# The head of a fused layer-norm, MLP and long-convolution kernel: activations rounded ahead of weights, three short matmuls, one filter block moved

## The chip, the cores and the metric

The kernel runs on one core of a Trainium2 chip. A core has a matrix engine (TensorE, PE in the profile, with its weight loads shown as PEld), a vector engine (DVE), a scalar engine (ACT), a general engine (POOL) and a sequencer for transfers (SP). Each works through its own instructions in order, and they wait for each other through semaphores. Data lie in the on-chip buffer, in the accumulators of TensorE (PSUM), or in DRAM; transfers are issued by SP, ACT or POOL. The metric is device time of one execution in microseconds, lower is better; before the change it is 369.86 us, the median of three runs (369.53 to 370.65).

## The reference

```python
x  = A_q                                            # 1 x 2048 x 448
xn = layernorm(x)
# A: short convolution over k (4 taps), times v, then a causal convolution of length 2048 by FFT
k_shift = sum(k_pad[:, t:t+S] * shift_k[:, 3 - t] for t in range(4))
kv = k_shift * v
y  = irfft(rfft(kv, 2S) * rfft(ssm_k, 2S))[:S] + kv * ssm_D
a  = xn * y
# B: dense, Mish, dense
h   = xn @ w1 + b1                                  # 448 -> 1792
act = h * tanh(softplus(h))
b   = act @ w2                                      # 1792 -> 448
out = x + a + b
```

All is in 32-bit floating point.

## The kernel before

**Matrix products in two parts.** TensorE takes operands rounded to a shorter format. Each operand is kept as a rounded part (names ending in h: XH, w1h, w2h, ach) and the remainder (XL, w1l, w2l, acl). ACT makes the rounded part by a cast, DVE makes the remainder by a subtraction. A product is the sum of three: rounded with rounded (hh), remainder of x with rounded w (hl), rounded x with remainder of w (lh). D = 448 is 3.5 blocks of 128, so for w1 the half block left over holds the remainder of w1 in the other 64 rows of `w1h[:, 3]` and adds two matmuls (th and tl). One half of a pair is thus 11 matmuls, and a pair 22.

**The MLP's loops.** The 2048 rows are cut in 8 chunks of 256, and the 1792 columns in 7 pairs of 128. The 56 pairs (chunk, column pair), numbered i, go through one pipeline of half steps s. An even half step, s = 2i, holds the first product of pair i (`g1_mm`, L486). An odd one holds its activation (`mish`, L494 and the splitting at L80 and L81) and the second product of the pair two before (`g2_mm`, twelve matmuls, L511 to L513). In the first chunk the weights are also loaded and split: column pair p of w1 in half step 2p - 2 (`w1_split`: L346 on ACT, L351 and L353 on DVE), that of w2 in half step 2p + 3 (`w2_split`).

**The convolution.** Its FFT is done by small matrix products. The filter is cut in 8 blocks h. A block is loaded (`h_load`, L117), goes through eight matmuls that take a stretch of the matrix engine (`f1_mm`, L131), is folded on ACT and DVE (`f1_fold`: L137, L138, L140) and is stored to DRAM (`f1_out`, L146). The table `H_AT` says in which half step the matmuls of each block but the head's stand. The head's block is block 1 (`H_HEAD`). The products of k and v follow in `KV_AT`, and second stages later.

**Order.** The program's order is written by hand (`manual_schedule`): `at(s, f)` puts work ahead of the matmuls of half step s, `after(s, f)` behind them; each engine takes its share in that order. Tiles come from pools with a fixed number of buffers: `kr` four, `x` seven, `pc` (PSUM) two, `st` two. A new tile waits until the buffer that it takes is free, and transfers share eight semaphores, so a transfer can wait for an older one that had the same semaphore.

**The head** (L635 to L680) comes before half step 0. TensorE does four matmuls of zeros (`WARM`, L643) while the first rows of q come in, these are normalized on DVE and POOL, transposed by TensorE (L446) into PSUM, and split: ACT casts XH (L458), DVE subtracts XL (L456). The first column pair of w1 comes in two halves of 128 columns (L652), one issued by ACT and one by SP, and is split in two halves. ACT first casts the first half of w1, then XH; DVE does the first half's remainder, then XL. Block 1 of the filter is loaded by ACT's queue at the start, block 2 by SP's; block 1's matmuls stand in half step 1, between the products of pair 0 and pair 1.

Of the kernel before, what the change touches and what calls it, by code (L numbers as in the profile page):

```python
# [14 lines left out]
S, D, F = 2048, 448, 1792  # L15
# [7 lines left out]

G2_LAG = 2
H_HEAD = 1
H_AT = {2: 5, 3: 9, 0: 12, 4: 16, 5: 20, 6: 26, 7: 32}
KV_AT = (24, 29, 34, 39, 44, 50, 55, 59)
POOL_H = {20: (0, 2)}
H0_AT = 63
# [4 lines left out]
NT_AT = {"q": -5, "x": -1, "stats": -2, "flush": 0, "row": (4, 8), "norm": (7, 10), "split": (8, 11)}  # L34
WARM = 4
WARM_N = 448


@with_exitstack
def tile_kernel(ctx: ExitStack, tc, q, qT, k, v, sk, hT, sD, w1, b1, w2, c_f1, c_id, c_g, c_gi, c_i2, out):  # L40
    nc = tc.nc
# [15 lines left out]
    Dh = dp.tile([NO * 16, 32, D], F32, name="Dh")  # L57
# [25 lines left out]
    def pc():  # L83
        return pcp.tile([128, 2, 512], F32, name="pc")
# [10 lines left out]
    plan, plan2 = {}, {}  # L95

    def at(slot, fn, *args):
        plan.setdefault(int(slot), []).append((fn, args))

    def after(slot, fn, *args):  # L100
        plan2.setdefault(int(slot), []).append((fn, args))
# [5 lines left out]
    HT, KR, VT, KV, PP, PS, ST, SD = {}, {}, {}, {}, {}, {}, {}, []  # L107

    def xt():
        return sp1.tile([128, 2, D], F32, name="x", bufs=7)  # L110

    def kr():
        return sp1.tile([128, 4, CH], F32, name="kr", bufs=4)

    def h_load(g, eng=None):
        HT[g] = xt()
        (eng or nc.sync).dma_start(HT[g], hT[:, 2 * g:2 * g + 2])  # L117
        if g == 0:
            dt = xt()[0:1, 0]
            nc.sync.dma_start(dt, sD)  # L120
            SD.append(dt)
# [217 lines left out]
    RW = {}  # L339
# [5 lines left out]
    def w1_hi(p, a=0, b=256):  # L345
        nc.scalar.copy(w1h[:, :, 256 * p + a:256 * p + b], RW["1", p][:, :, a:b])  # L346

    def w1_lo(p, a=0, b=256, engs=(V, V)):
        fs, rw = slice(256 * p + a, 256 * p + b), RW["1", p][:, :, a:b]
        if engs[0]:  # L350
            engs[0].tensor_sub(w1l[:, :, fs], rw[:, 0:3], w1h[:, 0:3, fs])  # L351
        if engs[1]:
            engs[1].tensor_sub(w1h[64:128, 3, fs], rw[64:128, 3], w1h[64:128, 3, fs])  # L353
# [3 lines left out]
        w1_lo(p)  # L357

    def w2_load(p):
        RW["2", p] = rw = kr().rearrange("p a b -> p (a b)")[:, :2 * D].rearrange("p (a b) -> p a b", a=2)  # L360
        nc.sync.dma_start(rw, w2[:, 2 * p:2 * p + 2])

    def w2_split(p):
# [16 lines left out]
    def ln_parts(c):  # L380
        st = mp.tile([128, 2, 6], F32, name="bst", bufs=2)
        ve = mp.tile([128, 2], F32, name="ve", bufs=2)
        if c < NT:
            XN[c] = xn = xn_tile().rearrange("p a b -> p (a b)").rearrange("p (j d) -> p j d", j=2)
        eng = nc.gpsimd if 0 < c < NCHUNK - 1 else V

        def stats(jj):
            V.bn_stats(st[:, jj], Q[c][:, jj])

        def aggr(jj):  # L390
            V.bn_aggr(mv[:, 2 * c + jj], st[:, jj])

        def eps(a, b):
            V.tensor_scalar(ve[:, a:b], mv[:, 2 * c + a:2 * c + b, 1], EPS, None, op0=ALU.add)  # L394

        def power(a, b):
            nc.gpsimd.tensor_tensor(rs(c)[:, a:b], ve[:, a:b], mhalf[:, a:b], op=ALU.pow)  # L397

        def norm(jj):
            j = 2 * c + jj  # L400
            eng.tensor_scalar(xn[:, jj, :D], Q[c][:, jj], mv[:, j, 0:1], rs(c)[:, jj:jj + 1],  # L401
                              op0=ALU.subtract, op1=ALU.mult)

        def tail(a, b):
            eng.tensor_copy(xn[:, a:b, D:], xn[:, a:b, D - 64:D])

        return stats, aggr, eps, power, norm, tail
# [36 lines left out]
    def transposes(c, jj, p):  # L444
        for kt in range(4):
            nc.tensor.transpose(p[:, 128 * kt:128 * kt + 128], XN[c][:, jj, 128 * kt:128 * kt + 128], ident)  # L446
# [5 lines left out]
    def x_split(c, jj, p, lo):  # L452
        x = p.rearrange("p (a b) -> p a b", a=4)
        h, l = (t[:, :, 128 * jj:128 * jj + 128] for t in XS[c])
        if lo:
            V.tensor_sub(l, x, h)  # L456
        else:
            nc.scalar.copy(h, x)  # L458
# [14 lines left out]
    def g1_mm(i):  # L473
        c, p = pairs[i]
        XH, XL = XS[c]
        ps = g1p.tile([128, 2, CH], F32, name="pg1")
        for n in range(2):
            f = 2 * p + n
            fs = slice(128 * f, 128 * f + 128)
            mm = []  # L480
            hh, hl, lh = ([(w[:, kt, fs], x[:, kt]) for kt in range(3)] for w, x in ((w1h, XH), (w1h, XL), (w1l, XH)))
            th, tl = ((w1h[:, 3, fs], x[:, 3]) for x in (XH, XL))

            mm = hh + hl + lh + [th, tl] if i == 0 and n else hh + lh + [th] + hl + [tl]
            for n_, (l, r) in enumerate(mm):
                nc.tensor.matmul(ps[:, n], l, r, start=n_ == 0, stop=n_ == len(mm) - 1)  # L486
        P1[i] = ps
# [38 lines left out]
    def mlp_slot(s):  # L526
        i, half = divmod(s, 2)
        n = len(pairs)
        j = i - G2_LAG
        if half == 0:  # L530
            if i < n:
                c, p = pairs[i]
                if c + 1 < NT:
                    if p == 0:
                        ln_load(c + 1)
                    if p == (3 if c in (0, 2) else 2):
                        ln_stats(c + 1)
                    if c == 0:
                        dv(len(drip))
                    if p == NP - 1:  # L540
                        ln_T(c + 1, 1)
                g1_mm(i)
        else:
            if i < n:
                c, p = pairs[i]
                if p == NP - 2 and c + 1 < NT:
                    ln_T(c + 1, 0)
                mish(i)
            if 0 <= j < n - 1:
                g2_mm(j)  # L550
            elif j == n - 1:
                for jj in range(2):
                    g2_mm(j, (jj,))
                    g2_evac(pairs[j][0], (jj,))
# [3 lines left out]
    nslots = 2 * (len(pairs) + G2_LAG)  # L558

    for g, t in H_AT.items():  # L560
        if g != 2:
            at(t - 5 if t > 7 else t - 3, h_load, g)
        if g == 0:
            after(t - 2, lambda: V.tensor_add(HT[0][0:1, 0], HT[0][0:1, 0], SD.pop()))
        at(t, f1_mm, HT, g, "h")
        if t in POOL_H:
            after(t, taps_pool, *POOL_H[t])
        after(t, f1_fold, g, "h")
        at(t + 3, f1_out, Dh, g, "h", nc.gpsimd if t < 12 else nc.scalar)

    at(12, lambda: nc.sync.dma_start(skb, sk.partition_broadcast(128)))
    for g in range(-2, 0):
# [13 lines left out]
    for p in range(NP):  # L586
        if p >= 2:
            at(max(2 * p - 5, 0), w1_load, p)
        if p >= 1:
            at(2 * p - 2, w1_split, p)  # L590
        p and at(2 * p + (1 if p < 5 else 0), w2_load, p)
        after(2 * (p + G2_LAG) - 1, w2_split, p)

    for o in range(NO):
        s, d = OCT_AT[0] + OCT_AT[1] * o, OCT_AT[1]
        h = s - 1 if o else H0_AT
# [23 lines left out]
    for c in range(NT, NCHUNK):  # L620
        b = 2 * NP * (c - 1) + (1 if c == NT else 0)
# [16 lines left out]
    wz = cp.tile([128, 8], F32, name="wz")  # L638
# [3 lines left out]
    for _ in range(WARM):  # L642
        nc.tensor.matmul(warm[0:8, 0:WARM_N], wz, wz[:, 0:1].to_broadcast([128, WARM_N]), start=True, stop=True)  # L643

# [5 lines left out]
    nc.scalar.dma_start(ident, c_id)  # L650
    for n, eng in enumerate((nc.scalar, nc.sync)):
        eng.dma_start(RW["1", 0][:, :, 128 * n:128 * n + 128], w1[0, :, :, 128 * n:128 * n + 128])  # L652
    h_load(H_HEAD, nc.scalar)
    nc.scalar.dma_start(f1, c_f1)
    w1_load(1)
    nc.sync.dma_start(b1t, b1)
    w2_load(0)
    h_load(2)
    stats, aggr, eps, power, norm, tail = ln_parts(0)
    for jj in range(2):  # L660
        stats(jj)
        aggr(jj)
        eps(jj, jj + 1)
        power(jj, jj + 1)
    w1_hi(0, 0, 128)
    ps = [g2p.tile([128, 512], F32, name="pg2") for _ in range(2)]
    x_tiles(0)
    for jj in range(2):
        norm(jj)
        tail(jj, jj + 1)  # L670
        transposes(0, jj, ps[jj])
        x_split(0, jj, ps[jj], 0)
    w1_lo(0, 0, 128)
    w1_hi(0, 128, 256)
    x_split(0, 0, ps[0], 1)
    x_split(0, 1, ps[1], 1)
    w1_lo(0, 128, 256)
    plan.setdefault(1, []).insert(0, (f1_mm, (HT, H_HEAD, "h")))
    plan2.setdefault(1, []).append((f1_fold, (H_HEAD, "h")))
    plan.setdefault(4, []).insert(0, (f1_out, (Dh, H_HEAD, "h", nc.gpsimd)))  # L680
    for s in range(nslots):
        j = s // 2 - G2_LAG - 1
        if s % 2 == 0 and j >= 0 and pairs[j][1] == NP - 1:
# [76 lines left out]
```

## Time and profile before

| | |
|---|---|
| median of three runs | 369.86 us |
| profiled execution | 370.36 us |
| its span, first to last instruction | 368.5 us |
| TensorE busy | 358.9 us, 97% |
| DVE busy | 268.1 us, 73% |
| ACT busy | 166.6 us, 45% |
| first product (L486) starts | 9.32 us |
| last 3.5 us of the span | no matmul |

In the profile a row of the timeline gives start, duration, engine, line, operation, written tile and read tiles, their shapes, the number of merged instructions, and in brackets the idle time before and what ended it. Matmuls overlap: one of 256 columns lasts 0.28 us in the records while the next starts 0.118 us after it. Rows of waits give the waiting engine, tile and line, who released it, total us, count, and the longest. The granted clock is a share of TensorE's full clock.

### The profile page before, as it was taken

How to read it: one execution, taken by the hardware profiler on the slowest of the kernel's cores; microseconds unless marked ns; L12 is line 12 of the kernel's file. 1: busy time of each engine (PE TensorE's matmuls, PEld its weight loads, DVE VectorE, ACT ScalarE, POOL GpSimd, SP SyncE). 2: the span in 40 equal slices, each digit the busy share in tenths (PEclk: the TensorE clock that was granted, in tenths of full speed). 3: DMA queues.
4: the chain of work that ended last, by engine and by line, in shares of the span. 5: the costliest groups of instructions: out<-in, count | busy, mean ns of one | idle time of the engine just before them, and what ended most of it. 6: DMA issues, size and time to landing. Idle time of an engine off the chain costs nothing.

```text
span 368.5 us, 7457 instructions
## 1 busy us (share of the span) xinstructions
PE 358.9 (97%) x3104; PEld 291.7 (79%) x3104; DVE 268.1 (73%) x368; ACT 166.6 (45%) x277; POOL 71.0 (19%) x65
## 2 busy tenths in 40 slices
PE   6989999999999999999999999999999999999996
PEld 1878879888789889889886666666666889889885
DVE  4698767899999898699525773777666644997752
ACT  3668454243342532433436663655656444135450
POOL 2015300750226420904000020000010005103020
PEclk9899999999999999999999999999999999999999
DMA  6888998848589157552888888998898387959656
GB/s 218 317 233 308 362 348 230 246 148 276 150 224 302 51 151 206 164 137 46 225 241 276 265 210 213 307 245 221 290 259 220 59 251 242 408 212 287 116 63 136
DMA packets 33508, 81.69 MB, mean 222 GB/s; under 512 B 3266, under 2 KB 20291, under 8 KB 33475
## 3 DMA queue, kind: packets, MB, share of 16 engines
q1 hardware_dynamic: 21506, 46.45, 37.9%
q10 hardware_dynamic: 9056, 20.09, 22.4%
q0 software_dynamic: 2912, 14.69, 13.8%
q8 instruction: 24, 0.39, 0.4%
q14 instruction: 10, 0.07, 0.1%
HBM read 52.77 MB, written 28.45 MB: 220 GB/s over the span
## 4 chain that ended last, share of the span: by engine, by line
PE 53%; DVE 2%; ACT 1%; ACTq 1%; issue 0%
PE pg L486 20%; PE pg L511 7%; PE pc L214 7%; PE pg L513 7%; PE pg L512 7%; PE pc L257 4%; PE pc L314 2%; ACTq L268 1%; DVE x L178 1%; PE pc L131 1%; DVE x L181 0%; ACT qe L265 0%; ACT a L494 0%; ACT hs L225 0%; DVE qt L518 0%
## 5 line engine op out<-in xcount | busy, mean ns | idle before, releaser
L494 ACT ACTIVATE a<-pg,b1t 128x256 f32<-128x256 f32 x112 | 47.1, 472 | 109.8 <-PE pg L486 96.3
L486 PE MATMUL pg<-XH,w1h 128*128 128x256 f32 x448 | 91.6, 286 | 1.7 <-ACT XH L458 1.5
L486 PEld LDWEIGHTS pg<-XH,w1h 128*128 128x128 f32 x448 | 70.3, 189 | 19.5 <-issue 16.5
L511 PE MATMUL pg<-w2h,ach 128*128 128x448 f32 x224 | 83.3, 372 | 0.0
L81 DVE TENSOR_TENSOR acl<-a,ach 128x512 fp32r<-128x512 f32 x56 | 39.1, 698 | 59.0 <-ACT ach L80 59.0
L512 PE MATMUL pg<-w2l,ach 128*128 128x448 f32 x224 | 81.3, 363 | 0.5 <-DVE w2l L81 0.5
L513 PE MATMUL pg<-w2h,acl 128*128 128x448 f32 x224 | 81.4, 363 | 0.0
L486 PE MATMUL pg<-XL,w1h 128*128 128x256 f32 x448 | 70.5, 280 | 0.2 <-DVE XL L456 0.2
L486 PEld LDWEIGHTS pg<-XL,w1h 128*128 128x128 f32 x448 | 60.3, 190 | 0.4 <-DVE XL L456 0.4
L486 PE MATMUL pg<-XH,w1l 128*128 128x256 f32 x336 | 57.3, 279 | 1.4 <-DVE w1l L351 1.4
L511 PEld LDWEIGHTS pg<-w2h,ach 128*128 128x128 f32 x224 | 42.0, 187 | 15.1 <-issue 12.2
L486 PEld LDWEIGHTS pg<-XH,w1l 128*128 128x128 f32 x336 | 47.2, 189 | 1.6 <-DVE w1l L351 1.6
L512 PEld LDWEIGHTS pg<-w2l,ach 128*128 128x128 f32 x224 | 42.1, 188 | 3.2 <-DVE w2l L81 0.8
L513 PEld LDWEIGHTS pg<-w2h,acl 128*128 128x128 f32 x224 | 42.1, 188 | 2.7
L80 ACT CAST ach<-a 128x512 fp32r<-128x512 f32 x56 | 34.7, 620 | 1.8
L161 POOL TENSOR_TENSOR x<-kr,skb 128x896 f32<-128x896 f32 x8 | 17.0, 2130 | 78.0 <-DVE x L160 53.8
L178 DVE TENSOR_TENSOR x<-x 128x896 f32<-128x896 f32 x24 | 26.3, 1096 | 2.7 <-POOL x L161 2.2
L397 POOL TENSOR_TENSOR mv<-ve,mhalf 128x2 f32<-128x2 f32 x3 | 3.7, 1249 | 97.9 <-DVE ve L394 97.9
L138 DVE TENSOR_TENSOR st<-pc,st 128x896 f32<-128x896 f32 x16 | 17.4, 1089 | 6.0 <-ACT st L137 5.3
L137 ACT COPY st<-pc 128x896 f32<-128x896 f32 x16 | 14.5, 906 | 15.7 <-PE pc L131 13.0
L401 POOL TENSOR_SCALAR xn<-qt,mv,rstd 128x448 f32<-128x448 f32 x8 | 20.7, 2591 | 0.4
L265 ACT COPY qe<-pc 128x896 f32<-128x896 f32 x16 | 13.8, 912 | 12.0 <-PE pc L257 11.8
(76 smaller groups left out, 399.6 us busy)
## 6 DMA issues: line engine op xcount, KB each, us to landing
Dkv<-st ACTq DMA_DIRECT2D x16, 448.0 KB, 6.2
ah<-Dh SPq DMA_DIRECT2D x8, 896.0 KB, 7.6
av<-Dkv SPq DMA_DIRECT2D x8, 896.0 KB, 6.7
E<-qe ACTq DMA_DIRECT2D x16, 448.0 KB, 5.6
e<-E POOLq DMA_DIRECT2D x8, 896.0 KB, 8.1
kr<-in_k_dram SPq DMA_DIRECT2D x10, 448.0 KB, 6.5
Dh<-st ACTq DMA_DIRECT2D x10, 448.0 KB, 5.3
x<-in_v_dram SPq DMA_DIRECT2D x8, 448.0 KB, 4.0
```

The lines of the kernel that those rows point to most:

```text
L80: nc.scalar.copy(h, raw)
L81: V.tensor_sub(l, raw, h)
L138: V.tensor_add(st[:, 0], e, st[:, 1])
L161: nc.gpsimd.tensor_mul(o, KR[g - u // 2], skb[:, u:u + 1].to_broadcast([128, 2, D]))
L178: V.tensor_add(KV[g], KV[g], o)
L214: nc.tensor.matmul(p[32 * t:32 * t + 32, r, :D], g[rs, t, c], a[rs, t], start=True, stop=True, tile_position=(64 * r, 32 * t))
L401: eng.tensor_scalar(xn[:, jj, :D], Q[c][:, jj], mv[:, j, 0:1], rs(c)[:, jj:jj + 1], op0=ALU.subtract, op1=ALU.mult)
L486: nc.tensor.matmul(ps[:, n], l, r, start=n_ == 0, stop=n_ == len(mm) - 1)
L494: nc.scalar.activation(a[:, n], ps[:, n], AF.Mish, bias=b1t[:, 2 * p + n:2 * p + n + 1])
L511: nc.tensor.matmul(ps, ah[:, n, cs], w2h[:, f], start=f == 0, stop=False)
L512: nc.tensor.matmul(ps, ah[:, n, cs], w2l[:, f], start=False, stop=False)
L513: nc.tensor.matmul(ps, al[:, n, cs], w2h[:, f], start=False, stop=f == NF - 1)
```

## The change

Four things move, and one is added.

- In the head XH is cast ahead of w1's first half on ACT, and XL comes ahead of w1's remainders on DVE. The first half of pair 0 takes the order hh, hl, lh that only the second half had.
- Three matmuls of zeros, of 224 columns, are put between the transposes and the first product (`FILL`, `FILL_N`). They write a `pc` tile that nothing reads.
- Block 1 is loaded by SP, where block 2 was; its matmuls stand in half step 3 instead of 1, its fold at the end of half step 3, its store in half step 5 instead of 4.
- Block 2 goes from half step 5 to 6, and is loaded in half step 3 instead of in the head; the stores of blocks 2 and 3 are issued two half steps behind their matmuls and not three.
- The loads of the last two pieces of w2 (p of 5 and 6) take buffers of the `x` pool, the others those of `kr`.

```diff
-H_AT = {2: 5, 3: 9, 0: 12, 4: 16, 5: 20, 6: 26, 7: 32}
+H_AT = {2: 6, 3: 9, 0: 12, 4: 16, 5: 20, 6: 26, 7: 32}
...
+FILL = 3
+FILL_N = 224
...
     def w2_load(p):
-        RW["2", p] = rw = kr().rearrange("p a b -> p (a b)")[:, :2 * D].rearrange("p (a b) -> p a b", a=2)
+        RW["2", p] = rw = xt() if p > 4 else kr().rearrange("p a b -> p (a b)")[:, :2 * D].rearrange("p (a b) -> p a b", a=2)
         nc.sync.dma_start(rw, w2[:, 2 * p:2 * p + 2])
...
-            mm = hh + hl + lh + [th, tl] if i == 0 and n else hh + lh + [th] + hl + [tl]
+            mm = hh + hl + lh + [th, tl] if i == 0 else hh + lh + [th] + hl + [tl]
...
-        if g != 2:
+        if g != H_HEAD:
             at(t - 5 if t > 7 else t - 3, h_load, g)
...
-        at(t + 3, f1_out, Dh, g, "h", nc.gpsimd if t < 12 else nc.scalar)
+        at(t + (2 if t < 12 else 3), f1_out, Dh, g, "h", nc.gpsimd if t < 12 else nc.scalar)
...
-    h_load(H_HEAD, nc.scalar)
     nc.scalar.dma_start(f1, c_f1)
     w1_load(1)
     nc.sync.dma_start(b1t, b1)
     w2_load(0)
-    h_load(2)
+    h_load(H_HEAD)
...
-    w1_hi(0, 0, 128)
     ps = [g2p.tile([128, 512], F32, name="pg2") for _ in range(2)]
     x_tiles(0)
...
         transposes(0, jj, ps[jj])
         x_split(0, jj, ps[jj], 0)
+    fill = pc()[:, 0]
+    for _ in range(FILL):
+        nc.tensor.matmul(fill[0:8, 0:FILL_N], wz, wz[:, 0:1].to_broadcast([128, FILL_N]), start=True, stop=True)
+    w1_hi(0, 0, 128)
+    x_split(0, 0, ps[0], 1)
+    x_split(0, 1, ps[1], 1)
     w1_lo(0, 0, 128)
     w1_hi(0, 128, 256)
-    x_split(0, 0, ps[0], 1)
-    x_split(0, 1, ps[1], 1)
     w1_lo(0, 128, 256)
-    plan.setdefault(1, []).insert(0, (f1_mm, (HT, H_HEAD, "h")))
-    plan2.setdefault(1, []).append((f1_fold, (H_HEAD, "h")))
-    plan.setdefault(4, []).insert(0, (f1_out, (Dh, H_HEAD, "h", nc.gpsimd)))
+    plan.setdefault(3, []).insert(0, (f1_mm, (HT, H_HEAD, "h")))
+    plan2.setdefault(3, []).append((f1_fold, (H_HEAD, "h")))
+    plan.setdefault(5, []).insert(0, (f1_out, (Dh, H_HEAD, "h", nc.gpsimd)))
```

On TensorE, from the second four transposes on, the order before is this (pg_172 is the accumulator of pair 0, pg_221 of pair 1; the row of L131 is block 1):

```order
L446 MATMUL pg_141<-idr,xn 128x128 x4
L486 MATMUL pg_172<-XH,w1h 128x256 x3
L486 MATMUL pg_172<-XH,w1l 128x256 x3
L486 MATMUL pg_172<-XH,w1h 128x256
L486 MATMUL pg_172<-XL,w1h 128x256 x4
L486 MATMUL pg_172<-XH,w1h 128x256 x3
L486 MATMUL pg_172<-XL,w1h 128x256 x3
L486 MATMUL pg_172<-XH,w1l 128x256 x3
L486 MATMUL pg_172<-XH,w1h 128x256
L486 MATMUL pg_172<-XL,w1h 128x256
L131 MATMUL pc<-x,f_81 64x448 x8
L486 MATMUL pg_221<-XH,w1h 128x256 x3
```

and in the changed kernel (lines stand two lower; pg_174 is pair 0):

```order
L448 MATMUL pg_138<-idr,xn 128x128 x4
L675 MATMUL pc<-wz 8x224 x3
L488 MATMUL pg_174<-XH,w1h 128x256 x3
L488 MATMUL pg_174<-XL,w1h 128x256 x3
L488 MATMUL pg_174<-XH,w1l 128x256 x3
L488 MATMUL pg_174<-XH,w1h 128x256
L488 MATMUL pg_174<-XL,w1h 128x256
```

The three matmuls of zeros stand ahead of pair 0, whose first half now takes XL ahead of w1l; block 1 has left its place behind pair 0 and stands behind pair 1.

On DVE, from the remainder of w1 for pair 1 on, the order before (L138 and L140 are the fold of block 1, L351 and L353 the remainder of w1, L81 that of an activation or of w2):

```order
L351 TENSOR_TENSOR w1l<-kr,w1h 128x3x256
L353 TENSOR_TENSOR w1h<-kr,w1h 64x256
L81 TENSOR_TENSOR acl<-a,ach 128x512
L138 TENSOR_TENSOR st<-pc,st 128x896
L140 TENSOR_TENSOR st<-pc,st 128x896
L351 TENSOR_TENSOR w1l<-kr,w1h 128x3x256
L353 TENSOR_TENSOR w1h<-kr,w1h 64x256
L81 TENSOR_TENSOR acl<-a,ach 128x512
L81 TENSOR_TENSOR w2l<-kr,w2h 128x896
```

and now:

```order
L353 TENSOR_TENSOR w1l<-kr,w1h 128x3x256
L355 TENSOR_TENSOR w1h<-kr,w1h 64x256
L83 TENSOR_TENSOR acl<-a,ach 128x512
L353 TENSOR_TENSOR w1l<-kr,w1h 128x3x256
L355 TENSOR_TENSOR w1h<-kr,w1h 64x256
L83 TENSOR_TENSOR acl<-a,ach 128x512
L83 TENSOR_TENSOR w2l<-kr,w2h 128x896
L140 TENSOR_TENSOR st<-pc,st 128x896
L142 TENSOR_TENSOR st<-pc,st 128x896
L353 TENSOR_TENSOR w1l<-kr,w1h 128x3x256
```

The fold of block 1 has moved from ahead of the remainder of w1 for pair 2 to ahead of that for pair 3.

On SP's queue, from the first piece of w2 on, with the semaphores waited for (DMAHW0 to 7 tell of landings). Before, 128x1024 being the weights of pairs 2 and 3, and x block 2:

```order
L361 DMA kr<-in_w_dram 128x896 [waits DMAHW0_49]
L117 DMA x<-in_hT_dram 128x896 [waits DMAHW2_49]
L343 DMA kr<-in_w_dram 128x1024 [waits DMAHW3_49]
L372 DMA qt<-in_q_dram 128x896 [waits DMAHW4_49]
L343 DMA kr<-in_w_dram 128x1024 [waits DMAHW5_49,DVE_49,Activation_49]
L361 DMA kr<-in_w_dram 128x896 [waits DMAHW6_49,DVE_49,Activation_49]
```

and now, the first x being block 1 and the second block 2:

```order
L363 DMA kr<-in_w_dram 128x896 [waits DMAHW0_49]
L119 DMA x<-in_hT_dram 128x896 [waits DMAHW1_49]
L345 DMA kr<-in_w_dram 128x1024 [waits DMAHW2_49]
L374 DMA qt<-in_q_dram 128x896 [waits DMAHW3_49]
L345 DMA kr<-in_w_dram 128x1024 [waits DMAHW4_49,DVE_49,Activation_49]
L119 DMA x<-in_hT_dram 128x896 [waits DMAHW5_49]
L363 DMA kr<-in_w_dram 128x896 [waits DMAHW6_49,DVE_49,Activation_49]
```

DMAHW1 tells here of the second half of q, DMAHW2 of the second half of the first weights. In before block 2 waited for DMAHW2 and the weights of pair 2 stood behind it; now block 1 waits for DMAHW1 only, and the weights of pair 2 for DMAHW2.

## The prediction

> **What bounds the kernel now.** I read the page's engine shares first, then TensorE's own waits, then its busy time by stage, and last the head row by row.
>
> ```profile
> span 368.5 us, 7457 instructions
> PE 358.9 (97%) x3104; PEld 291.7 (79%) x3104; DVE 268.1 (73%) x368; ACT 166.6 (45%) x277; POOL 71.0 (19%) x65
> ```
>
> TensorE (PE) is busy for 358.9 of 368.5 us, so only its idle 9.6 us, and time in which it runs slowly, can be won. Its waits by releaser, with total, count and longest:
>
> ```profile
> PE pg L486 <- ACT XH L458: 1.5, 1, 1.5
> PE pg L486 <- DVE w1l L351: 1.4, 1, 1.4
> PE pg L512 <- DVE w2l L81: 0.5, 1, 0.5
> PE pg L486 <- DVE XL L456: 0.4, 2, 0.2
> ```
>
> By stage (columns: busy us and count of PE, weight load, DVE, ACT, POOL; then granted clock, DMA share, GB/s):
>
> ```profile
> 0.00:23.00 23.00, 17.89 (x115) 11.62 (x115) 14.68 (x30) 12.15 (x19) 3.65 (x9) 0.93 0.76 238
> 23.00:60.00 37.00, 36.46 (x279) 32.34 (x272) 27.07 (x36) 21.99 (x35) 8.66 (x9) 1.00 0.91 328
> 60.00:162.00 102.00, 101.84 (x783) 90.20 (x781) 93.69 (x133) 36.98 (x69) 37.30 (x22) 1.00 0.67 190
> 162.00:365.00 203.00, 202.73 (x1938) 157.57 (x1938) 132.08 (x171) 95.50 (x156) 21.35 (x25) 1.00 0.76 218
> ```
>
> The first 23 us hold 5.1 us of idle PE and all of the reduced clock; the 342 us from 23 to 365 hold 0.97 us of idle. What PE gains in the head therefore reaches the end one for one, as long as DVE and the loads move with it. The head on PE:
>
> ```profile
> 9.32 0.62 PE L486 MATMUL pg<-XH,w1h 128*128 128x256 f32 x3 [1.54 <-ACT XH L458]
> ...
> 10.58 1.22 PE L486 MATMUL pg<-XL,w1h 128*128 128x256 f32 x4 [0.18 <-DVE XL L456]
> ...
> 14.00 1.01 PE L131 MATMUL pc<-x,f 32*64 32x448 f32 x16
> 14.94 0.62 PE L486 MATMUL pg<-XH,w1h 128*128 128x256 f32 x3
> ...
> 17.64 0.58 PE L486 MATMUL pg<-XH,w1h 128*128 128x256 f32 x3
> 19.57 0.62 PE L486 MATMUL pg<-XH,w1l 128*128 128x256 f32 x3 [1.35 <-DVE w1l L351]
> ...
> 22.05 1.01 PE L131 MATMUL pc<-x,f 32*64 32x448 f32 x16
> 22.99 0.47 PE L511 MATMUL pg<-w2h,ach 128*128 128x448 f32 x1
> ...
> 25.51 0.52 PE L486 MATMUL pg<-XH,w1h 128*128 128x256 f32 x3
> ```
>
> So pair 0 takes 9.32 to 14.00 (4.68 us), block 1 of the filter 0.94, pair 1 takes 14.94 to 17.64 (2.70), pair 2 17.64 to 22.05 (4.41). All three pairs are the same 22 matmuls; pair 1 neither waits nor is slowed, so 2.70 is what a pair costs (0.118 a matmul and 0.1 at its start). Pair 0 is long because its last 15 matmuls, from 10.58 to 14.00, take 0.228 each. The clock says why:
>
> ```profile
> 3.61:7.03 3.42, 2.50 (x9) 0.69 (x7) 2.96 (x9) 0.00 (x0) 1.30 (x2) 1.00 0.71 200
> 7.03:10.44 3.41, 1.70 (x11) 1.30 (x11) 2.24 (x5) 2.21 (x4) 0.00 (x0) 1.00 1.01 373
> 10.44:13.85 3.41, 3.27 (x15) 3.27 (x15) 2.22 (x5) 1.04 (x1) 0.00 (x0) 0.50 0.92 306
> ```
>
> After a stretch of 3.41 us in which PE was busy half the time (1.70), the next 3.41 us were granted half the clock; after one with 2.50 of 3.42 it stayed full.
>
> **The change part by part.** The durations on ACT (ScalarE) and DVE that I use:
>
> ```profile
> 7.68 0.62 ACT L346 CAST w1h<-kr 128x512 fp32r<-128x512 f32 x1 [5.45 <-DMA kr<-in_w_dram]
> 8.20 1.07 ACT L458 CAST XH<-pg 128x512 fp32r<-128x512 f32 x2
> 9.66 0.62 ACT L346 CAST w1h<-kr 128x512 fp32r<-128x512 f32 x1 [0.39 <-DMA kr<-in_w_dram]
> 10.97 1.04 ACT L346 CAST w1h<-kr 128x1024 fp32r<-128x1024 f32 x1 [0.69 <-DMA kr<-in_w_dram]
> 14.11 0.84 ACT L494 ACTIVATE a<-pg,b1t 128x256 f32<-128x256 f32 x2 [2.09 <-PE pg L486]
> 14.98 0.62 ACT L80 CAST ach<-a 128x512 fp32r<-128x512 f32 x1
> ...
> 16.49 1.05 ACT L346 CAST w1h<-kr 128x1024 fp32r<-128x1024 f32 x1
> ```
>
> ```profile
> 8.33 0.56 DVE L351 TENSOR_TENSOR w1l<-kr,w1h 128x384 fp32r<-128x384 f32 x1 [1.09 <-ACT w1h L346]
> ...
> 9.24 1.29 DVE L456 TENSOR_TENSOR XL<-pg,XH 128x512 fp32r<-128x512 f32 x2
> ...
> 12.05 0.96 DVE L351 TENSOR_TENSOR w1l<-kr,w1h 128x768 fp32r<-128x768 f32 x1 [0.74 <-ACT w1h L346]
> ...
> 16.44 1.09 DVE L138 TENSOR_TENSOR st<-pc,st 128x896 f32<-128x896 f32 x1
> ...
> 20.61 1.08 DVE L81 TENSOR_TENSOR w2l<-kr,w2h 128x896 fp32r<-128x896 f32 x1
> ```
>
> *XH first.* The transposes end at 7.78 (9.32 less the idle 1.54). XH's second piece then runs 7.83 to 8.37, w1's first 128 columns (landed at 7.68) 8.37 to 8.95 or so, and the first product starts at 9.00 instead of 9.32. XL now precedes w1's remainder on DVE, one piece of 0.65 behind each XH piece, so done at 9.07; the XL matmuls of the new order are wanted at 9.45. w1l's first piece is done at 9.65 (wanted 9.81); w1's second half, even if it lands at 9.66 as now, is rounded at 10.28 (wanted 10.40) and its w1l done at 10.85 (wanted 11.1). No wait is left in pair 0: it ends at 9.00 + 2.70 = 11.70 at full clock.
>
> *Three short matmuls.* Their speed is read from the weight loads of the warm-up's last matmuls at full clock:
>
> ```profile
> 4.16 0.09 PEld L643 LDWEIGHTS pg<-wz 128*8 128x8 f32 x1 [0.29 <-issue]
> 4.54 0.09 PEld L643 LDWEIGHTS pg<-wz 128*8 128x8 f32 x1 [0.29 <-issue]
> ```
>
> 0.38 a record, eight records for four matmuls of 448 columns; 224 columns are half, so three cost 3 x 2 x 0.19 = 1.14 us, 7.78 to 8.93, inside what is idle. They delay nothing before 9.00; with the cover gone they would cost up to 1.1 us. What they do is fill the stretch 7.03 to 10.44: 0.6 of transposes, 1.14, and 1.4 of products make 3.1 of 3.41 us, above the 2.50 that kept the clock. I take it that the clock stays full. [...]
>
> *Block 1 in half step 3.* Its 0.94 us of PE moves behind pair 1, and its fold (two DVE operations of 1.09 and one on ACT) behind the remainder of w1 for pair 2 and of w2 for pair 0. The 1.35 us wait at 19.57 came from that fold standing ahead of w1l. So pair 2 needs 2.70, not 4.41. Without new waits the head's ledger is 9.00 + 2.70 + 2.70 + 0.94 + 2.70 = 18.04 where before has 22.05: **4.0 us** gained.
>
> What is late next? First, pair 1's weights. Block 1 no longer loads on ACT's queue at the start, so 448 KB fewer go ahead; at the 373 GB/s of the second clock row that is 1.2 us. The load lands between 9.8 and the present 10.97; I take 10.2, nearer the early end since the block now comes after it. Rounded 11.25, w1l done 12.25, wanted at 12.15: with a restart 0.3 us lost (0 to 1.0).
>
> Second, pair 2's weights. Their load still waits for the first weights' second half to land. What the change takes from ahead of it is block 2's load.
>
> ```profile
> x<-in_hT_dram SPq DMA_DIRECT2D x1, 448.0 KB, 5.6
> ```
>
> That is block 2's load, the one issued in that place before (9.65). Issued at about 8.9 (from 8.0 to 9.66), pair 2's weights land 5.6 later at 14.5; ACT is free then (pair 0's activations and rounding, 0.84 and 0.62 from 11.75, end at 13.2). Rounded 15.55, w1l done at 16.55, wanted at 16.1: 0.6 us lost. The ends are 0 and 2.5 (rounding at 16.49 as now, w1l at 18.6).
>
> Third, the moved fold. Pair 1 ends near 14.7; activation, rounding, acl, w2h and w2l bring DVE to about 18.3, the fold to 20.5, pair 3's w1l to 21.5. PE wants the fold's PSUM for block 2 after pair 2 (18.9) and twelve second-product matmuls (22.99 to 25.51, 2.5), at 21.4, and that w1l at 22.8. Covered by 0.9 and 1.3 us; beyond that each us of delay is one of PE, and everything behind it.
>
> *w2's last pieces.* They leave the four kr buffers for two of seven x buffers, free at that time. The wait on w2l (0.5) is bound to this stage:
>
> ```profile
> 47.06 0.91 ACT L137 COPY st<-pc 128x896 f32<-128x896 f32 x1 [2.72 <-DMA Dh<-st]
> ```
>
> There ACT stands 2.72 us on a store of an earlier block, with piece 5 of w2 queued behind. POOL issues that store; it is tied to DVE, which moves about as PE does. Gain 0 to 0.8 (the wait and a restart), taken as 0.3. Block 2's load, now behind pair 3's weights on SP, and block 3's store, a half step earlier on POOL's queue, cost nothing visible: block 2 is wanted on PE only at 21.4, and the store waits for its fold either way.
>
> Sum: 4.0 - 0.3 - 0.6 + 0.3 = 3.4 us. The profiled execution took 370.36 (span and 1.9 around it), so 367.0; the median 369.86 is 0.5 lower, so 366.5.
>
> **The rivals.**
>
> *The clock still halves for one stretch.* For it: the short matmuls use eight weight columns, and what counts as activity is not shown. Against: the warm-up is the same kind and brought the full clock. Half of 3.41 us, 1.7, is lost, but then PE reaches the two new waits late and they vanish: 3.4 - 1.7 + 0.9 = 2.6 gained, 367.3. [...]
>
> *Loads as late as now.* Pair 1's weights at 10.97, pair 2's rounded at 16.49: 1.0 and, of 2.5, the 1.8 not already spent; 4.0 - 1.0 - 1.8 + 0.3 = 1.5 gained, 368.4. For it: four transfers are outstanding at once there. Against: 448 KB less is ahead of both.
>
> *The lead is refilled.* DVE is busy 93.69 of 102 us from 60 to 162. Were it to start that stretch no earlier, PE would wait there instead: 369.9. Against it: its operations wait for PE and for loads that PE's progress frees.
>
> *Block 1 lands late (slower).* Its load moves from ACT's queue at 2.02 to SP's, behind the weights of pairs 0 and 1 and w2's first piece, and waits for the second half of q, as the filter constants' load did:
>
> ```profile
> 4.45 0.33 ACTq L654 DMA_DIRECT2D f<-in_c_f_dram  x1
> ```
>
> PE reaches block 1 at about 14.7 and every later product stands behind it. Landing at 18.1 eats the gain; after 19.2 the kernel is slower by 0.3%. Landing 15.4 us after its issue, at 19.9, makes 369.86 + 1.8 = 371.7. The longest median among loads of this size is that of k:
>
> ```profile
> kr<-in_k_dram SPq DMA_DIRECT2D x2, 448.0 KB, 9.9
> ```
>
> That would be 14.3, in time.
>
> **How the numbers follow.** Forecast 0.62, clock 0.13, late loads 0.13, lead refilled 0.05, block late 0.07. The first three are faster (0.88), the fourth the same (0.05), the last slower (0.07); 0.3%, about 1.1 us, is what a measurement tells from no change. The likeliest case runs from 365.1 (no new waits and all of the w2l wait: 4.8 gained) to 367.3; with the clock and the late loads the range is 365.1 to 368.5, which leaves out the last two cases, 0.12, and some tail.
>
> **What would show it.** Full clock from 3.61 on; the first product near 9.0; block 1 on PE near 14.7 to 15; no wait of L351's kind near 1.4 us, but one of up to 1 us in pair 2; pair 2 done near 19. The prediction is wrong if PE's gain at 25 us is not 3 to 4 us, or if idle PE appears after 23 us that before did not have.

## The result and the profile after

The changed kernel takes 365.85 us, the median of six runs (365.45 to 367.06), and the kernel before on the same chip 369.53 (367.53 to 370.65). The ratio is 0.9912, with a 95% interval of 0.9882 to 0.9941: faster by 0.9%, 3.7 us. Forecast were 366.5, in a range of 365.1 to 368.5. The profiled execution took 366.62, 3.74 less than the profiled one of before. Four executions of the kernel before, of 372.8 to 373.9 us, were in a slower state and are left out of every median and ratio below. Lines of `kernel.py` now stand two further down: L488 is the first product, L513 to L515 the second, L133 a filter block, L353 w1's remainder, L460 XH.

The page of the changed kernel, its span and engine shares:

```profile
span 364.8 us, 7468 instructions
PE 359.5 (99%) x3110; PEld 290.6 (80%) x3110; DVE 268.1 (73%) x368; ACT 166.0 (46%) x277; POOL 71.0 (19%) x65
```

TensorE is busy 0.6 us longer in a span 3.7 shorter. The three short matmuls add 1.3 us, and the eight records of the warm-up last 5.92 us where they lasted 4.46; pair 0 at full clock takes away. The list of its waits (releaser, total, count, longest):

```profile
PE pg L645 <- DVE wz L641: 1.0, 1, 1.0
PE pg L514 <- DVE w2l L83: 0.4, 1, 0.4
PE pc L216 <- ACT hs L227: 0.2, 1, 0.2
PE pg L488 <- DVE XL L458: 0.2, 1, 0.2
```

The 1.5 us on XH and the 1.4 on w1l are gone; the 0.5 on w2l is 0.4. By stage, in the columns of before's table:

```profile
0.00:23.00 23.00, 22.02 (x141) 13.91 (x142) 15.88 (x32) 14.93 (x23) 3.65 (x9) 1.00 0.87 288
23.00:60.00 37.00, 36.62 (x281) 32.57 (x280) 29.40 (x40) 19.47 (x33) 8.81 (x9) 1.00 0.91 318
60.00:162.00 102.00, 101.81 (x794) 89.44 (x792) 93.73 (x132) 37.48 (x70) 37.24 (x22) 1.00 0.65 187
162.00:361.00 199.00, 198.80 (x1906) 154.72 (x1900) 128.43 (x166) 94.15 (x153) 21.31 (x25) 1.00 0.77 220
```

In the first 23 us the granted clock reads 1.00 with 0.98 us idle (before 0.93 and 5.1). The record of the clock begins only at 6.55 us; ahead of that the warm-up's matmuls take 0.74 us a record, against 0.38 at full clock. Behind 23 us the idle is 0.77 (0.97 before). The timeline of TensorE in the head:

```profile
7.85 1.31 PE L675 MATMUL pc<-wz 128*8 128x224 f32 x6
9.17 0.62 PE L488 MATMUL pg<-XH,w1h 128*128 128x256 f32 x3
...
11.94 0.52 PE L488 MATMUL pg<-XH,w1h 128*128 128x256 f32 x3
...
14.64 1.01 PE L133 MATMUL pc<-x,f 32*64 32x448 f32 x16
15.58 0.62 PE L488 MATMUL pg<-XH,w1h 128*128 128x256 f32 x3
...
18.52 0.36 PE L513 MATMUL pg<-w2h,ach 128*128 128x448 f32 x1
...
21.02 1.01 PE L133 MATMUL pc<-x,f 32*64 32x448 f32 x16
21.95 0.62 PE L488 MATMUL pg<-XH,w1h 128*128 128x256 f32 x3
```

Pair 0 now takes 2.77 us (4.68 before), pair 1 2.70, block 1 0.94, pair 2 2.94 (4.41 before). Pair 2 ends at 18.52 where it ended at 22.05: 3.53 us. When the matmuls of both traces are laid side by side, the lead is 3.5 us at 25 us, still 3.5 at 47, 3.7 behind the wait on w2l and 3.7 at the end (361.2 and 365.0). It reached the end one for one.

On DVE the head's fold now stands behind the remainder of w1 that pair 2 needs:

```profile
15.10 0.96 DVE L353 TENSOR_TENSOR w1l<-kr,w1h 128x768 fp32r<-128x768 f32 x1 [0.74 <-ACT w1h L348]
...
17.34 1.09 DVE L83 TENSOR_TENSOR w2l<-kr,w2h 128x896 fp32r<-128x896 f32 x1
18.35 1.08 DVE L140 TENSOR_TENSOR st<-pc,st 128x896 f32<-128x896 f32 x1
19.47 1.09 DVE L142 TENSOR_TENSOR st<-pc,st 128x896 f32<-128x896 f32 x1
20.47 0.95 DVE L353 TENSOR_TENSOR w1l<-kr,w1h 128x768 fp32r<-128x768 f32 x1
```

And the loads have moved. The trace has the second half of the first weights landed at 7.95 us (9.64 before), pair 1's weights at 9.10 (10.95), pair 2's at 14.0 (16.47), and block 1 at 11.36 (9.46). The rows of the second half of the first weights and of block 1, with size and us from issue to landing, before:

```profile
kr<-in_w_dram SPq DMA_DIRECT2D x1, 256.0 KB, 8.0
x<-in_hT_dram ACTq DMA_DIRECT2D x1, 448.0 KB, 7.4
```

and now:

```profile
kr<-in_w_dram SPq DMA_DIRECT2D x1, 256.0 KB, 6.3
x<-in_hT_dram SPq DMA_DIRECT2D x1, 448.0 KB, 7.0
```

### The profile page after: what moved, and what is told of

It is laid out like the page before. It is cut to its first block, busy times and chain, and to the rows that moved or that the text cites. A ratio compares the mean times of both kernels' runs of the same rounds, so it can differ in the third digit from the quotient of the medians.

```text
span 364.8 us, 7468 instructions
## 1 busy us (share of the span) xinstructions
PE 359.5 (99%) x3110; PEld 290.6 (80%) x3110; DVE 268.1 (73%) x368; ACT 166.0 (46%) x277; POOL 71.0 (19%) x65
## 4 chain that ended last, share of the span: by engine, by line
PE 54%; DVE 2%; ACT 1%; ACTq 1%; issue 0%
PE pg L488 20%; PE pg L513 7%; PE pc L216 7%; PE pg L515 7%; PE pg L514 7%; PE pc L259 4%; PE pc L316 2%; ACTq L270 1%; DVE x L180 1%; PE pc L133 1%; DVE x L183 0%; ACT qe L267 0%; ACT a L496 0%; ACT hs L227 0%; DVE qt L520 0%
## 5 line engine op out<-in xcount | busy, mean ns | idle before, releaser
L488 PE MATMUL pg<-XH,w1h 128*128 128x256 f32 x448 | 91.1, 285 | 0.2 <-DVE XL L458 0.2
L488 PEld LDWEIGHTS pg<-XH,w1h 128*128 128x128 f32 x448 | 69.7, 188 | 18.8 <-issue 15.8
L513 PE MATMUL pg<-w2h,ach 128*128 128x448 f32 x224 | 83.2, 371 | 0.0
L515 PE MATMUL pg<-w2h,acl 128*128 128x448 f32 x224 | 81.4, 363 | 0.0
L488 PE MATMUL pg<-XL,w1h 128*128 128x256 f32 x448 | 69.7, 277 | 0.0
L488 PEld LDWEIGHTS pg<-XL,w1h 128*128 128x128 f32 x448 | 59.5, 188 | 0.0
L488 PE MATMUL pg<-XH,w1l 128*128 128x256 f32 x336 | 57.0, 278 | 0.0
L513 PEld LDWEIGHTS pg<-w2h,ach 128*128 128x128 f32 x224 | 42.0, 187 | 14.4 <-issue 11.5
L488 PEld LDWEIGHTS pg<-XH,w1l 128*128 128x128 f32 x336 | 46.9, 188 | 0.1
L515 PEld LDWEIGHTS pg<-w2h,acl 128*128 128x128 f32 x224 | 42.1, 188 | 2.6
L139 ACT COPY st<-pc 128x896 f32<-128x896 f32 x16 | 14.5, 906 | 15.5 <-PE pc L133 13.0
L140 DVE TENSOR_TENSOR st<-pc,st 128x896 f32<-128x896 f32 x16 | 17.4, 1088 | 5.4 <-ACT st L139 5.2
```

Source lines behind the costliest of these rows:

```text
L140: V.tensor_add(st[:, 0], e, st[:, 1])
L513: nc.tensor.matmul(ps, ah[:, n, cs], w2h[:, f], start=f == 0, stop=False)
L515: nc.tensor.matmul(ps, al[:, n, cs], w2h[:, f], start=False, stop=f == NF - 1)
```

## The experiments

The main theory is the prediction's: XH first, the short matmuls and the moved fold each bring a part, and the short matmuls are what keeps the clock. The rival is that the clock and the early start come from the loads, because block 1's no longer goes on ACT's queue ahead of the rest. Diffs are against the changed kernel unless said otherwise. The experiments ran in three sets, each beside the kernel before. The first holds the four from "Without the short matmuls" to "Block 1's load back on ACT's queue", the second the repeat of the change and the three from "Without XH first" to "Block 2's store earlier", the third the last four. Medians of the kernel before were 369.59 us, 370.40 and 369.66. The ratios are to the kernel before of the same set; they differ from the quotients of these medians by up to 0.4%.

### The changed kernel again

No edit; it is the yardstick of the others.

> The changed kernel as it is, beside the others on the same chip. 365.5 to 366.5, every execution at full clock (mean granted clock 0.998 or more). It is the measure for the three others.

366.29 us (365.57 to 366.9), ratio 0.9899 (0.9872 to 0.9927). With the first six runs at 365.85, differences of 0.4 us between kernels say nothing.

### Without the short matmuls

```diff
-FILL = 3
+FILL = 0
```

> The changed kernel without its three short matmuls. Theory (the clock follows how busy PE was in the stretch of 3.41 us before): PE idles about 1.2 us between the transposes and the first product; a stretch that holds this idle and the gaps around the transposes has 1.3 to 2.0 us of work, near or under the 1.70 that was followed by half clock before the change. So the records show one stretch of 3.41 us at half clock, pair 0 or pair 1 runs at 0.21 to 0.23 us a matmul, and of the gain of 3.7 us over before 0.7 to 1.7 us is lost: 366.6 to 367.5. [...]

366.06 us (365.9 to 367.11), ratio 0.9871 (0.9827 to 0.9915): the time of the change. The mean granted clock is 0.998 or more in all six executions. The timeline and the windows of clock in this kernel:

```profile
8.91 0.62 PE L488 MATMUL pg<-XH,w1h 128*128 128x256 f32 x3 [1.19 <-ACT w1h L348]
```

```profile
7.77:11.19 3.42, 2.28 (x19) 2.28 (x20) 2.97 (x7) 2.56 (x4) 0.00 (x0) 1.00 1.01 393
```

TensorE idles 1.19 us ahead of the first product, not 1.54; the stretch with that idle holds 2.28 us of work, and the next keeps its clock. The theory's lost half stretch did not come. The short matmuls are not needed in the changed kernel.

### The short matmuls alone

This one is against the kernel before.

```diff
+FILL = 3
+FILL_N = 224
...
+    fill = pc()[:, 0]
+    for _ in range(FILL):
+        nc.tensor.matmul(fill[0:8, 0:FILL_N], wz, wz[:, 0:1].to_broadcast([128, FILL_N]), start=True, stop=True)
```

> The kernel before with the three short matmuls alone, between the transposes and the first product. Theory: the clock stays full after 7 us, pair 0 lasts near 2.9 us and not 4.68, but pair 1 then waits for its weights (rounded at 12.0) and pair 2 for the remainder of its own behind block 1's fold, so only 1.1 to 1.6 us of the time are gained: 368.0 to 368.5 where before has 369.5. Rival (the short matmuls have no part in the clock): half clock from about 10.4 on, no gain.

368.37 us (367.45 to 371.96), ratio 0.9953 (0.9918 to 0.9988). In the old order they are worth 1.7 us by the ratio (0.4 to 3.0 by its interval). Two of twelve executions still have a mean clock of 0.993 or 0.994, where nine of eighteen of the kernel before have one of 0.993 to 0.995. So they do not exclude a lost half stretch; that they make it rarer is likely, on few executions. The old wait on w1l is there:

```profile
PE pg L488 <- DVE w1l L353: 1.1, 1, 1.1
```

### Block 1's matmuls and fold back in half step 1

```diff
-    plan.setdefault(3, []).insert(0, (f1_mm, (HT, H_HEAD, "h")))
-    plan2.setdefault(3, []).append((f1_fold, (H_HEAD, "h")))
-    plan.setdefault(5, []).insert(0, (f1_out, (Dh, H_HEAD, "h", nc.gpsimd)))
+    plan.setdefault(1, []).insert(0, (f1_mm, (HT, H_HEAD, "h")))
+    plan2.setdefault(1, []).append((f1_fold, (H_HEAD, "h")))
+    plan.setdefault(4, []).insert(0, (f1_out, (Dh, H_HEAD, "h", nc.gpsimd)))
```

> The changed kernel with block 1's matmuls and fold back in half step 1 and its store in 4; all else as changed. Theory (the fold stood ahead of w1's remainder for pair 2 on DVE): DVE does acl, then the fold until about 16.7, then that remainder until 17.7, while PE wants it at 16.1; PE waits 1.3 to 1.7 us there and 1.0 to 1.6 us of the time are lost: 366.9 to 367.5. Rival (pair 2 waits for its load, landing at 14.0, whatever the fold does): the same as the change, 365.9.

367.76 us (366.76 to 368.71), ratio 0.9949 (0.9917 to 0.9982): 1.5 us over the repeat of the change, 1.7 over the kernel without short matmuls in the same set. Its timeline, DVE and then TensorE:

```profile
15.23 1.09 DVE L142 TENSOR_TENSOR st<-pc,st 128x896 f32<-128x896 f32 x1
16.23 0.95 DVE L353 TENSOR_TENSOR w1l<-kr,w1h 128x768 fp32r<-128x768 f32 x1
```

```profile
17.23 0.62 PE L488 MATMUL pg<-XH,w1l 128*128 128x256 f32 x3 [1.42 <-DVE w1l L353]
```

The fold ends, w1l starts behind it without a gap, and TensorE waits 1.42 us. ACT had w1h for it cast at 15.03, so the load did not hold it up. That the old wait came from the fold's place on DVE is shown: block 1's place is the only edit, and the wait returns with it.

### Block 1's load back on ACT's queue

```diff
+    h_load(H_HEAD, nc.scalar)
     nc.scalar.dma_start(f1, c_f1)
...
     w2_load(0)
-    h_load(H_HEAD)
```

> The changed kernel with block 1 loaded by ACT's queue ahead of the filter constants, as before the change; its matmuls stay in half step 3. Theory (that load goes ahead of the weights): the first weights' second half lands at 9.6 and not 7.95, pair 1's weights at 10.9 and not 9.1, pair 2's load is issued at 9.7 and not 7.96 and lands 1.2 to 1.7 us later; PE waits about 0.9 us in pair 1 and 0.5 to 1.2 us in pair 2, 1.0 to 2.0 us lost: 366.9 to 367.9. Rival (landings there are set by something else than what is ahead): the same as the change, 365.9.

367.23 us (366.97 to 368.08), ratio 0.9896 (0.9848 to 0.9944): 0.9 us over the repeat of the change, 1.2 over the kernel without short matmuls in the same set. The first weights' second half lands at 9.32, pair 1's at 10.64, pair 2's at 15.29. TensorE waits once each in pairs 1 and 2, less than the 0.9 and 0.5 to 1.2 expected:

```profile
12.76 0.62 PE L488 MATMUL pg<-XH,w1l 128*128 128x256 f32 x3 [0.37 <-DVE w1l L353]
...
17.40 0.62 PE L488 MATMUL pg<-XH,w1l 128*128 128x256 f32 x3 [0.38 <-DVE w1l L353]
```

The load's place is worth about 1 us with the short matmuls in. What follows is its worth without them.

### Without XH first

w1's first half is rounded ahead of XH again, with the old order of products in the first half of pair 0; the short matmuls stay.

```diff
+    w1_hi(0, 0, 128)
...
-    w1_hi(0, 0, 128)
-    x_split(0, 0, ps[0], 1)
-    x_split(0, 1, ps[1], 1)
     w1_lo(0, 0, 128)
     w1_hi(0, 128, 256)
+    x_split(0, 0, ps[0], 1)
+    x_split(0, 1, ps[1], 1)
...
-            mm = hh + hl + lh + [th, tl] if i == 0 else hh + lh + [th] + hl + [tl]
+            mm = hh + hl + lh + [th, tl] if i == 0 and n else hh + lh + [th] + hl + [tl]
```

> The changed kernel with w1's first half cast ahead of XH and its remainder ahead of XL, as before the change, and the old order hh, lh, hl in pair 0's first half; the short matmuls stay. Theory: the first product starts 0.2 to 0.4 us later and the XL matmuls wait 0.1 to 0.3, the clock stays full; 0.3 to 0.7 us lost against the change. Rival (the order of the casts is what keeps the clock, not the short matmuls): half clock in about half of the executions, 1 us and more lost in the median.

366.17 us (365.48 to 366.64), ratio 0.9897 (0.9869 to 0.9924): no loss. The first product starts at 8.93, behind the short matmuls as in the change (8.95 in the repeat); w1's first half lands near 6.97, so ACT has time for its cast ahead of XH. XH first buys nothing here.

### Neither XH first nor the short matmuls

The edit of "Without XH first" and `FILL = 0`. What is left of the change are the moved filter blocks, with block 1's load on SP's queue, and w2's pool.

> As the kernel with w1 first, and without the three short matmuls: the idle of 1.5 us before the first product is back, the loads and block 1 stay as changed. Theory (the clock follows how busy PE was in each stretch of 3.41 us, and either of the two, casts or short matmuls, lifts it enough): about half of the executions have a stretch at half clock (mean granted clock 0.993 to 0.995), as the kernel before had, and the median is 0.7 to 1.7 us above the change. Rival (the clock is kept by the moved block and the earlier weights): full clock in all, 0.3 to 0.5 us above the change.

365.95 us (365.34 to 366.22), ratio 0.9888 (0.9859 to 0.9917): again the time of the change, with a clock of 0.999 or more in all six executions. ACT's first weight cast and TensorE's first product in the timeline:

```profile
6.63 0.62 ACT L348 CAST w1h<-kr 128x512 fp32r<-128x512 f32 x1 [4.40 <-DMA kr<-in_w_dram]
```

```profile
8.49 0.62 PE L488 MATMUL pg<-XH,w1h 128*128 128x256 f32 x3 [0.68 <-ACT XH L460]
```

The weights that landed at 7.68 before are there at 6.63. The idle is 0.68 us, not 1.54, and needs no filling: in the 18 executions of the three kernels with the load on SP's queue and no short matmuls (this one, "Without the short matmuls" and "All that seemed to help") none has a mean clock under 0.998. The product starts 0.46 ahead of the repeat's; pair 0 then takes 2.87 against 2.60 there, because XL comes later, and at the second product 0.12 is left (17.83 and 17.95).

### Block 2's store earlier

The store of block 2 goes one half step ahead, and the statistics of the second chunk come one pair later, so that POOL issues the store before its work on the next rows and ACT's copy at 43 us need not stand for it.

```diff
-                    if p == (3 if c in (0, 2) else 2):
+                    if p == (4 if c == 0 else 3 if c == 2 else 2):
...
-        at(t + (2 if t < 12 else 3), f1_out, Dh, g, "h", nc.gpsimd if t < 12 else nc.scalar)
+        at(t + (1 if t == 6 else 2 if t < 12 else 3), f1_out, Dh, g, "h", nc.gpsimd if t < 12 else nc.scalar)
```

> The changed kernel with block 2's store one half step earlier and the second chunk's statistics one pair later, so that POOL issues that store ahead of the normalization and not behind it. Theory (ACT's stand of 2.6 us on that store's landing, at 43 us, makes the wait on w2l at 47.8): the store is issued near 28.7 and not 33.2, ACT's stand is gone or under 1 us, PE's wait of 0.4 with it, 0.3 to 0.7 us gained against the change. Rival (the store lands no earlier, since transfers there are limited by throughput, or the later normalization makes the transposes wait at 35.5): no gain, or up to 2 us lost.

366.32 us (365.62 to 366.79), ratio 0.99 (0.9873 to 0.9928). ACT's copy in the change, and here:

```profile
43.35 0.91 ACT L139 COPY st<-pc 128x896 f32<-128x896 f32 x1 [2.56 <-DMA Dh<-st]
```

```profile
40.26 0.91 ACT L139 COPY st<-pc 128x896 f32<-128x896 f32 x1
```

The wait on w2l of the change (0.6 in the repeat's trace) is gone from the list of waits with ACT's stand, which bears out that the stand was its cause; the last matmul ends at 360.3 and not 361.2 in the profiled executions. The medians do not show it (366.32 and 366.29): half a microsecond is what they scatter by.

### Neither XH first nor the short matmuls, and the load on ACT's queue

The edit above, and the one of "Block 1's load back on ACT's queue". What is left of the change are the later matmuls and folds of the filter blocks and w2's pool.

> The order of the kernel before in the head (w1 rounded ahead of XH, no short matmuls) with block 1's matmuls in half step 3, but its load back on ACT's queue ahead of the first weights. If it is the load's place that kept the clock in e9 (the first weights landed 1 us earlier, and the idle ahead of the first product was 0.68 us and not 1.5), then the idle comes back to 1.3 to 1.6 us, the first product starts at 9.2 to 9.4, pair 1's weights land at 10.5 to 11, about half of the executions read a mean clock of 0.993 to 0.995, and the median is 367.3 to 368.6: longer than e4 (367.23), which differs by the short matmuls and XH's place. The rival, that the moved matmuls alone keep the clock, expects no execution under 0.998 and 367.0 to 367.5, the time of e4.

368.19 us (366.81 to 369.69), ratio 0.9969 (0.9943 to 0.9996). From 365.95 this differs by the queue of one load: 2.2 us across two sets. In its own set it is 1.8 over "All that seemed to help" (366.38), which differs by the queue and by block 2's earlier store. Its rows:

```profile
8.14 0.62 ACT L348 CAST w1h<-kr 128x512 fp32r<-128x512 f32 x1 [5.91 <-DMA kr<-in_w_dram]
```

```profile
9.78 0.62 PE L488 MATMUL pg<-XH,w1h 128*128 128x256 f32 x3 [2.08 <-ACT XH L460]
```

```profile
5.42:8.83 3.41, 2.14 (x11) 0.93 (x9) 1.49 (x6) 0.69 (x2) 0.75 (x1) 1.00 1.01 341
8.83:12.24 3.41, 2.28 (x17) 2.08 (x18) 3.20 (x7) 2.46 (x4) 0.00 (x0) 1.00 0.93 324
12.24:15.65 3.41, 3.41 (x37) 3.28 (x44) 1.72 (x3) 2.25 (x4) 0.00 (x0) 1.00 0.85 320
```

The weights are 1.51 us later than with the load on SP's queue, the idle grows to 2.08 (more than the 1.3 to 1.6 expected), and in four of twelve executions the mean clock is 0.993 to 0.995 (a median of 368.8, against 367.8 for the other eight). The profiled one kept its clock; its idle lies across the border of two stretches, and each held over 2.1 us of work. Full clock was the rival's condition, and it fell. In the two profiled executions, both at full clock, the second product starts at 19.34 and 17.83, so 1.5 of the 2.2 us is plain lateness of the weights (1.1 of the 1.8 in the set's own pair, where it starts at 18.28).

### All that seemed to help

w1 ahead of XH, no short matmuls, and the earlier store.

> e9 and e8 in one kernel: w1 rounded ahead of XH, no short matmuls, and block 2's store ahead of POOL's normalization. First product at 8.4 to 8.6, no wait on w2l over 0.1 us near 50 us: if the two add up, 365.95 less 0.3 to 0.5, 365.4 to 365.7. The rival, that neither moves the end, expects 366.0 to 366.4 as the changed kernel.

366.38 us (365.47 to 366.99), ratio 0.9924 (0.9894 to 0.9954). The first product starts at 8.52 and no wait on w2l is left, but the median is the change's, as the rival said. No version is below the change by more than the scatter.

### The last pieces of w2 in the old pool

```diff
-        RW["2", p] = rw = xt() if p > 4 else kr().rearrange("p a b -> p (a b)")[:, :2 * D].rearrange("p (a b) -> p a b", a=2)
+        RW["2", p] = rw = kr().rearrange("p a b -> p (a b)")[:, :2 * D].rearrange("p (a b) -> p a b", a=2)
```

> The changed kernel with the last pieces of w2 in the pool where they were before. The prediction put the new pool at nothing, so this should give the time of the changed kernel within 0.3 us (366.0 to 366.6), the wait on w2l near 48 to 51 us unchanged at 0.4 to 0.6. The rival, that the new pool frees buffers that the key tiles waited for, expects 0.4 us or more on top, with waits of TensorE between 50 and 62 us that the changed kernel does not have.

366.64 us (365.39 to 367.05), ratio 0.9923 (0.9894 to 0.9952). The wait on w2l reads 1.0 us in the list of waits, where 0.4 to 0.6 was expected, and no other wait appears between 50 and 62 us. The median is 0.35 over the repeat, within the scatter: a gain of the new pool of some tenths is neither shown nor excluded.

### Six short matmuls

```diff
-FILL = 3
+FILL = 6
```

> Six short matmuls in place of three: each takes about 0.38 us of TensorE, so the first product starts at 10.0 to 10.2 in place of 9.0 to 9.2. If what the head loses reaches the end one for one, the median is 1.0 to 1.2 us over the changed kernel, 366.9 to 367.5. The rival, that later waits on weights absorb the delay, expects 0.3 us or less, 366.0 to 366.6, with the wait on w2l near 48 us gone.

367.30 us (366.34 to 367.81), ratio 0.9948 (0.9925 to 0.9971). Its timeline:

```profile
7.66 2.46 PE L675 MATMUL pc<-wz 128*8 128x224 f32 x12
10.05 0.62 PE L488 MATMUL pg<-XH,w1h 128*128 128x256 f32 x3
```

The product starts 1.10 later than the repeat's, the second product 0.94 later, and the median is 1.0 higher. What is put on TensorE in the head comes out at the end, nearly one for one. The wait on w2l stays (0.5).

## Why the prediction was right, and where it was not

**One for one.** Confirmed: by the lead through the trace, and by six short matmuls. The rival that DVE refills the lead from 60 to 162 us has nothing for it (0.19 us of idle there).

**Without new waits, 4.0 us.** The ledger's places were 9.00 for the first product and 18.04 for pair 2's end; the trace has 9.17 and 18.52.

**The half stretch at half clock.** The ledger was read off one execution of the kernel before, which had a mean clock of 0.995, and counted its loss whole: 1.7 us of the 4.0. Of the kernel's 53 other executions beside the experiments, 31 do not lose it, with a median of 368.86 us; the twelve of the changed kernel have 366.05. So some 2.8 us are gained with no clock in play, by these figures. In the second set, where both kernels ran side by side, it is 3.8 (370.07 and 366.29). The clock's part in the median is the smaller one, and that a ledger with the loss counted whole came out near the median was in part luck.

**Pair 1's weights, -0.3, and pair 2's, -0.6.** The direction was right, the losses too large. Landings were taken as 10.2 and 14.5 and came at 9.10 and 14.0. The first lies below the early end that was allowed (9.8), which took the load's bytes at 373 GB/s as all that its place could cost; the second load was issued at 7.96, at the early end of its range. Pair 1 lost nothing (2.70 us), pair 2 0.24 (2.94), pair 0 0.07 (2.77).

**w2l, +0.3.** The wait shortened from 0.54 to 0.38, and the lead grew by 0.2 there. The cause given, ACT's stand on a store, is borne out by the earlier store. The sum is then 3.53 and 0.2, 3.73 for 3.4 forecast.

**Block 1 in half step 3.** Shown by the experiment that puts it back. The moved fold ended at 20.56, 0.46 ahead of block 2's matmuls (0.9 forecast), and pair 3's w1l was done near 21.4, 1.0 ahead of its use (1.3 forecast). No wait came. Block 1 itself was in 3.3 us ahead of its matmuls, 7.0 us after its issue, so the slower rival was far off; no run shows the 15.4 us that it took for that load.

**Three short matmuls: the step that failed.** The prediction had them fill the stretch from 7.03 to 10.44 and concluded "that the clock stays full". They run as forecast (1.31 us with their start, 1.14 forecast) but the clock stays full without them, and XH first brings nothing either. The working took the first weights to land at 7.68 as before, though it had the block's load out of the way for pair 1's. They land at 6.6 to 7.0 where they can be seen (ACT's first cast with w1 ahead of XH). That leaves 0.7 to 1.2 us of idle, over which no execution lost its clock. With the load on ACT's queue the same two parts are worth about 1.0 us (368.19 to 367.23, in two sets): they are cover for late weights, and the change takes away the lateness as well. The number was right because the ledger's end, a pair 0 at full clock from about 9.0, holds by either way; for this term that is luck.

**"Full clock from 3.61 on".** The changed kernel's trace has full clock from 6.55. The stretches do not start with the kernel: their phase gave a first full stretch at 3.61 us in the trace of the kernel before, at 5.42 with neither XH first nor the short matmuls and the load on ACT's queue, and at 6.55 in the changed kernel. What held is that no later stretch lost it: in the 12 executions of the changed kernel the mean is 0.998 or more.

What stays open is the exact split of the 3.7 us between the fold, the earlier weights and the clock (the last two follow from the same load), and whether the new pool for w2 is worth anything. Two things are untested: the load's move alone in the kernel before, and by themselves, block 2's later place and the earlier stores of blocks 2 and 3.

## What to carry to other kernels

Before filling an idle stretch, ask what ends it: here a 448 KB load on another queue delayed the weights by 1.51 us (8.14 against 6.63), and moving it made the filling needless (a mean clock of 0.998 or more in all 18 executions with the load moved and no filling). Rounding work that a later product needs goes ahead of folding work that nobody waits for yet. And when a change has several parts, take each out of the finished kernel as well as adding it to the old one: the short matmuls are worth about 1.7 us in the old kernel (0.4 to 3.0) and nothing that shows in the new.

## What was not expected of the hardware

The kernel before has two kinds of execution. Of the 53 in the three sets, 22 have a mean clock of 0.993 to 0.995, with a median of 370.5 us, and 31 of 0.998 or more, with 368.9. The difference of 1.6 us is about half of one stretch of 3.41 us. That the same idle of about 1.5 us costs half a stretch or not by how it falls on the borders is the likely reading, but only one execution of this kernel has a trace. In the heads of the traces a stretch that held 1.70 us of work was followed by half clock (the kernel before, 7.03 to 10.44 us). One with 2.14 us and one with 2.28 kept it in the kernel with neither XH first nor the short matmuls and the load on ACT's queue (5.42 to 8.83 and 8.83 to 12.24 us), as did one with 2.28 in the changed kernel without the short matmuls (7.77 to 11.19). So a stretch need not be empty for the clock to halve behind it: that one held 1.70 us of work in 3.41. Whether busy time alone decides, and with what border, these four stretches do not show.

One load's queue moved others by about its share of the rate, or more. At the 373 GB/s of the prediction's clock row, 448 KB is 1.2 us. With ACT's first cast as the mark, the first half of the first weights was there at 6.63 us (neither XH first nor the short matmuls) and 6.97 (without XH first) with the load on SP's queue, and at 7.68 (the kernel before) and 8.14 (neither, and the load on ACT's queue) with it on ACT's: 1.1 us apart in the mean, and 1.51 between 6.63 and 8.14, which differ by the queue alone. The second half landed at 7.95 in the changed kernel, at 9.32 in the one that differs by the queue alone, and at 9.64 in the kernel before: 1.4 and 1.7 us later. By what mechanism a load on one queue holds up loads on another is not shown by these runs.
